# A linear-attention and feed-forward kernel: GpSimd's sums cut into parts, two casts on ScalarE, two sums and three stores moved

## The chip, the cores and the metric

One core of a Trainium2 chip runs the whole program. The metric is the time of one execution in microseconds on the device; three runs of the kernel before gave a median of 224.1 us (223.25 to 224.87). The profile is of one more execution, taken by the hardware profiler. The engines are named as the profile names them: PE is TensorE (matrix products; PEld is its weight loads), DVE is VectorE, ACT is ScalarE, POOL is GpSimd, and SP is SyncE, whose queue issues nearly all transfers.

## The reference, cut to what matters

```python
def _attn_ref(q, k, v, lam):                  # (4, 8, 768, 64) each, lam: one decay per head
    for b in range(nb):                       # blocks of 64 positions
        intra = einsum('bhic,bhjc->bhij', qb, kb) * Dmask      # decay lam**(i-j), causal
        intra = einsum('bhij,bhjd->bhid', intra, vb)
        inter = einsum('bhid,bhde->bhie', qb * lam_pow, kv_state)
        out[:, :, sl] = intra + inter
        kv_state = lam_block * kv_state + einsum('bhsd,bhse->bhde', kb_dec, vb)

def _moe_ref(x, w_a, w_b, w_out):             # x: 3072 tokens x 512, d_ff = 1536
    a = x @ w_a
    b = x @ w_b
    return a * b @ w_out
```

The attention's output, with its heads joined, is the x of the feed-forward part. Inputs and output are float32; the kernel multiplies in bfloat16.

## The kernel before, in words

The 3072 tokens are 24 units of 128 (four sequences of six blocks; the kernel takes blocks of 128). `GROUPS = (4, 1, 2, 4, 4, 4, 4, 1)` gathers them into eight groups, and the feed-forward part works on one group at a time. While it multiplies group g, the attention of later units is woven in, a piece at a time, at numbered slots. `PLAN[g]` lists by hand which piece goes at which slot of group g; `hook(slot)` emits them. What a piece's letters mean, as far as it matters here:

- `P`: prepare a unit. `prep_k` (L433) scales k and q by the decay on GpSimd (L411) and has SP issue the transpose by DMA (L439); `prep_v` (L444) casts v to bfloat16 on the engine that `VB_ENG` names (L428, L430) and then calls `pump` (L312), which lets SP issue the loads of a later unit. `PK` and `PV` are the two halves.
- `S`, `O2`, `V`: the scores of a unit with their masks (L467, L481, L482, L490), the outputs of two units (L507; L530 writes them to xT, the feed-forward part's input) and the update of the state.
- `W`: `store_kept` (L637) has SP store one of five early output rows that were kept in SBUF (L639). Rows 3 and 4 lie in one tile, rows 0, 1 and 2 in another, with the tag `zab`.
- `X`: `x_sums` (L730) forms for the next group the three sums z_sub, z_add and z_mix of quarters of xT.
- `SM`: `ab_sum` (L852), one of eight partial sums of a group's product tile `ab`. The sums go to a tile z with the tag `zab`, the same memory as the kept rows 0 to 2, or back into `ab`.
- `H`: `out_half` (L873), half of one product of the output.

Groups 3 to 6 use seven products in place of eight for each pair of blocks (`ffn_z`, L752): every product's operands are quarters of xT and of the weights, or their sums. A round n of six forms the seven products for one slice of columns of both a and b: product 1 goes to a PSUM bank U, 4 to a bank V, 5 and 2 or 3 add onto U, 6 onto V, and 0 goes to W. Product 4 reads z_sub, 5 reads z_mix, 6 and 0 read z_add, and product 2, the last, reads z_sub. ScalarE copies U and V to SBUF (L849), and DVE subtracts (L797, L805, L807, L809, L814). L807 must have read U before product 2 adds onto it (`last_product`, L772), which is done one round later; then ScalarE casts U (L774) and DVE multiplies a by b into rows n and n + 6 of `ab` (L776). A round has three slots, 3n to 3n + 2; at slot 3n + 1 of groups 3 and 4 the last product of round n - 1 has just been issued. In group 5 and 6 the outputs of the group before run at the same time (`joined`), and the last product of round n - 1 follows right after product 1.

`ab_sum(4, 0)` adds two column halves of rows 0 to 2 of `ab` (into z3), `ab_sum(4, 2)` subtracts in place in rows 0 to 2, reading rows 6 to 8 as well, and `ab_sum(4, 4)` goes on from it. `SUM_ENG` gives sum (4, 0) to DVE and (4, 2) to GpSimd; of the 24 sums of groups 4 to 6, GpSimd has 13, each of 3 x 256 elements a partition. `XS_ENG` gives z_add and z_mix of group 5 and all three sums of group 6 to GpSimd (1024, 1024 and 512 elements).

Every engine takes its instructions in the order in which they were issued, and so does SP's queue: a piece that waits holds all that stands behind it on its engine.

Of the kernel before, what the change touches and what calls it, by code (L numbers as in the profile page):

```python
# [22 lines left out]
def _bc(ap, dims):  # L23
# [73 lines left out]
VB_ENG = dict(enumerate(["pool"] * 7 +  # L97
                        ["dve"] * 3 +
                        ["pool"] * 5 +
                        ["dve"] * 2 +  # L100
                        ["act"] +
                        ["pool"] +
                        ["dve"] +
                        ["pool"] +
# [1 line left out]
SUM_ENG = {(3, 0): 'dve', (3, 1): 'dve', (3, 2): 'pool', (3, 3): 'dve', (3, 4): 'pool', (3, 5): 'pool', (3, 6): 'dve', (3, 7): 'dve', (4, 0): 'dve', (4, 1): 'pool', (4, 2): 'pool', (4, 3): 'pool', (4, 4): 'dve', (4, 5): 'pool', (4, 6): 'pool', (4, 7): 'pool', (5, 0): 'dve', (5, 1): 'dve', (5, 2): 'pool', (5, 3): 'pool', (5, 4): 'dve', (5, 5): 'pool', (5, 6): 'pool', (5, 7): 'dve', (6, 0): 'pool', (6, 1): 'dve', (6, 2): 'pool', (6, 3): 'dve', (6, 4): 'dve', (6, 5): 'pool', (6, 6): 'dve', (6, 7): 'dve'}  # L106
XS_ENG = {(3, 0): 'dve', (3, 1): 'dve', (3, 2): 'dve', (4, 0): 'dve', (4, 1): 'dve', (4, 2): 'dve', (5, 0): 'dve', (5, 1): 'pool', (5, 2): 'pool', (6, 0): 'pool', (6, 1): 'pool', (6, 2): 'pool'}
# [6 lines left out]
def kernel(  # L114
# [12 lines left out]
    B, H, S, D = q.shape  # L127
# [7 lines left out]
    KS = d_model // 128  # L135
# [61 lines left out]
    HN, NP = d_model // 2, FC // 2  # L197
# [209 lines left out]
    def eng_of(name):  # L407
        return nc.gpsimd if name == "pool" else nc.vector
# [314 lines left out]
    def x_tile():  # L723
        return xz_pool.tile([128, 2, 512], BF16, name="z_add", tag="xz")
# [5 lines left out]
    def x_sums(g):  # L730
        xT = gx[g]
        z_add = x_first.pop(g) if g in x_first else x_tile()
        add_half = lambda c: nc.vector.tensor_add(z_add[:, :, c], xT[:, 0:2, c], xT[:, 2:4, c])
        z_sub = xz_pool.tile([128, KS, 256], BF16, name="z_sub", tag="xz")
        z_mix = mix_pool.tile([128, 2, 256], BF16, name="z_mix", tag="z_mix")
        xz[g] = (z_add, z_sub, z_mix)
        if g == Z_GROUPS[0]:
            sub = lambda s: nc.vector.tensor_sub(z_sub[:, s], xT[:, s, 0:256], xT[:, s, 256:512])
            sub(slice(0, 2))
            nc.vector.tensor_add(z_mix, xT[:, 0:2, 0:256], xT[:, 2:4, 256:512])  # L740
            add_half(slice(256, 512))
            sub(slice(2, 4))
            return
        eng_of(XS_ENG[g, 0]).tensor_sub(z_sub, xT[:, :, 0:256], xT[:, :, 256:512])
        eng_of(XS_ENG[g, 1]).tensor_add(z_add, xT[:, 0:2, :], xT[:, 2:4, :])
        eng_of(XS_ENG[g, 2]).tensor_add(z_mix, xT[:, 0:2, 0:256], xT[:, 2:4, 256:512])

    fin = []
    pairs = [0]
    outs = {}  # L750
# [101 lines left out]
    def ab_sum(g, i):  # L852
        d = outs[g]
        if "z" not in d:
            d["z"] = sum_pool.tile([128, 2, NP, 256], BF16, name="zab", tag="zab")
        ab, z, j, h = d["ab"], d["z"], i // 2, i % 2
        lo, hi = h * NP // 2, (h + 1) * NP // 2
        a11, a12 = ab[:, lo:hi, :256], ab[:, NP + lo:NP + hi, :256]
        a21, a22 = ab[:, lo:hi, 256:], ab[:, NP + lo:NP + hi, 256:]
        z1, z3 = z[:, 0, lo:hi], z[:, 1, lo:hi]  # L860
        eng = eng_of(SUM_ENG[g, i])
        if j == 0:
            eng.tensor_add(z3, a11, a21)
        elif j == 1:
            eng.tensor_sub(a21, a22, a21)
        elif j == 2:
            eng.tensor_sub(z1, a11, a21)
        else:
            eng.tensor_sub(z1, a12, z1)
# [165 lines left out]
    for g, n in enumerate(GROUPS):  # L1035
# [6 lines left out]
        def hook(slot, plan=plan):  # L1042
            for name, us in plan.get(slot, ()):
# [9 lines left out]
                elif name == "W":  # L1053
                    store_kept()
                elif name == "WS":
                    weight_sum(us)
                elif name == "WO":
                    out_sum(us)
                elif name == "SM":
                    ab_sum(*us)  # L1060
                elif name == "H":
                    out_half(*us)
                elif name == "XA":
                    x_add_first(us)
                elif name == "X":
                    x_sums(us)
                elif name == "T":
                    piece_T(us)
                elif name == "S":
                    piece_S(us)  # L1070
                elif name == "VC":
                    kv_copy(us, kv["ps"], KV_ENG[us])
                elif name == "V":
                    piece_V(us)
                elif name == "O":
                    pieces_O((us,))
                elif name == "O2":
                    pieces_O(us)
                else:
                    pieces_O(us[:2], us[2:])  # L1080
# [41 lines left out]
```

## Time and profile before

| | us |
|---|---|
| median of three runs | 224.1 |
| the profiled execution | 223.99 |
| its span, first to last instruction | 222.3 |
| PE busy | 214.2 |
| DVE busy | 166.1 |
| ACT busy | 122.2 |
| POOL busy | 101.4 |
| PE waits on named engines from 82 us on (1.0, 0.3, 0.3, and some of 0.2) | about 2 |

Busy time is the union of an engine's instructions, and the granted clock of TensorE is 1.00 throughout. A line of a timeline reads: start, duration, engine, line of the code, operation, output and input, count; in brackets the idle time of that engine just before, and what ended it. Group 4's rounds run from about 117 to 141 us, group 5's to about 171, group 6's to about 202.

### The profile page before, as it was taken

Reading aid. Unit: us, or ns where it says so; the run is one execution under the profiler, and the core shown is the slowest. Engines: PE = TensorE matmul, PEld = TensorE weight load, DVE = VectorE, ACT = ScalarE, POOL = GpSimd, SP = SyncE. Lnnn points to the kernel's source line nnn. Section 1 sums busy time; section 2 is a strip of 40 time slices with the busy share of each in tenths; the row PEclk is TensorE's granted clock in tenths of the full one; section 3 lists DMA queues with packets and bytes.
Section 4 is the critical chain, followed back from the end, with each engine's and each line's share of the span. In section 5 each row is a group of like instructions: output and inputs, shape, how many; then the busy total and the mean of one; then the engine's idle time right before and its main releaser. Section 6 shows DMA issues by size and latency. Waiting matters only on the chain.

```text
span 222.3 us, 5600 instructions
## 1 busy us (share of the span) xinstructions
PE 214.2 (96%) x2225; PEld 158.8 (71%) x2235; DVE 166.1 (75%) x272; ACT 122.2 (55%) x249; POOL 101.4 (46%) x99
## 2 busy tenths in 40 slices
PE   7799999999999999999999999899999999999994
PEld 2376444448788658886547888688888888888994
DVE  0895673987868667989999879968688865777540
ACT  2586447028454267664356988676635566543322
POOL 6052003337795365533479519786417722051100
PEclk9999999999999999999999999999999999999999
DMA  3999999999999999999999999872021100112042
GB/s 107 332 245 354 354 386 355 272 222 208 223 196 190 217 188 232 192 288 186 193 254 195 266 230 254 140 131 49 1 86 59 52 0 3 49 47 97 0 145 94
DMA packets 99081, 39.42 MB, mean 177 GB/s; under 512 B 85488, under 2 KB 95088, under 8 KB 99056
## 3 DMA queue, kind: packets, MB, share of 16 engines
q1 hardware_dynamic: 98768, 39.00, 80.5%
q8 instruction: 17, 0.28, 0.6%
q10 hardware_dynamic: 288, 0.07, 0.1%
q14 instruction: 8, 0.07, 0.1%
HBM read 28.32 MB, written 6.29 MB: 156 GB/s over the span
## 4 chain that ended last, share of the span: by engine, by line
PE 68%; DMA 14%; DVE 8%; SPq 3%; issue 3%; ACT 2%; ACTq 0%; DVEq 0%
PE U L768 17%; PE op L890 12%; PE V L768 9%; DMA wst<-in_moe_w_b_dram 8%; PE op L655 5%; PE W L768 5%; PE a_ps L606 5%; PE b_ps L606 5%; PE o_ps L507 3%; DMA kf<-in_k_dram 3%; DMA k<-in_k_dram 3%; PE op L830 3%; PE kq L467 2%; DVE m L490 2%; SPq L360 1%
## 5 line engine op out<-in xcount | busy, mean ns | idle before, releaser
L849 ACT COPY u<-U 128x512 f32<-128x512 f32 x48 | 28.4, 591 | 17.3 <-PE U L768 17.3
L411 POOL TENSOR_TENSOR qk<-kf,lp_k 128x512 bf16<-128x512 f32 x18 | 20.2, 1124 | 26.3 <-DMA kf<-in_k_dram 19.9
L633 DVE TENSOR_TENSOR ab<-a_sb,b_ps 128x128 bf16<-128x128 bf16 (+2 forms) x48 | 19.5, 418 | 15.4 <-ACT a_sb L615 11.0
L776 DVE TENSOR_TENSOR ab<-oab 128x1024 bf16<-128x1024 bf16 x24 | 20.4, 848 | 10.7 <-ACT oab L774 10.5
L606 PE MATMUL b_ps<-xT,wb_sb 128*128 128x128 bf16 (+2 forms) x192 | 27.5, 272 | 0.2 <-DVE wb_sb L251 0.2
L606 PE MATMUL a_ps<-xT,wa_sb 128*128 128x128 bf16 (+2 forms) x198 | 27.4, 267 | 0.1
L490 DVE TENSOR_TENSOR m<-kq,lotri 128x512 bf16<-128x512 f32 x40 | 25.6, 680 | 0.9 <-PE kq L467 0.8
L615 ACT CAST a_sb<-a_ps 128x128 bf16<-128x128 f32 (+2 forms) x48 | 17.1, 375 | 13.8 <-PE a_ps L606 13.1
L411 POOL TENSOR_TENSOR qk<-qf,lp_q 128x512 bf16<-128x512 f32 x20 | 23.0, 1149 | 2.6 <-DMA qf<-in_q_dram 2.1
L655 PE MATMUL op<-wo_sb,ab 128*128 128x512 bf16 (+2 forms) x114 | 22.0, 335 | 0.5 <-issue 0.3
L606 PEld LDWEIGHTS <-wa_sb 128*128 128x128 bf16 x200 | 16.7, 98 | 6.0 <-POOL wa_sb L246 0.2
L768 PEld LDWEIGHTS <-wz_a 128*128 128x128 bf16 x192 | 18.1, 98 | 3.6 <-issue 0.3
L768 PEld LDWEIGHTS <-wz_b 128*128 128x128 bf16 x192 | 18.7, 98 | 2.2
L606 PEld LDWEIGHTS <-wb_sb 128*128 128x128 bf16 x192 | 15.7, 98 | 6.3 <-DVE wb_sb L251 0.3
L530 ACT CAST xT<-o_ps 128x512 bf16<-128x512 f32 (+1 forms) x24 | 12.2, 554 | 12.8 <-PE o_ps L507 12.7
L768 PE MATMUL U<-xT,wz_a 128*128 128x256 bf16 x96 | 18.3, 272 | 0.0
L768 PE MATMUL U<-xT,wz_b 128*128 128x256 bf16 x96 | 18.3, 272 | 0.0
L430 POOL CAST vb<-vf 128x512 bf16<-128x512 f32 x14 | 10.1, 724 | 17.0 <-DMA vf<-in_v_dram 14.6
L768 PEld LDWEIGHTS <-wa_sb 128*128 128x128 bf16 x144 | 13.4, 98 | 4.6 <-issue 1.8
L807 DVE TENSOR_TENSOR oab<-U,u 128x512 bf16<-128x512 f32 x24 | 16.3, 680 | 0.6 <-PE U L768 0.6
L774 ACT CAST oab<-U 128x512 bf16<-128x512 f32 x24 | 14.2, 591 | 3.9 <-PE U L768 3.9
L655 PEld LDWEIGHTS <-ab 128*128 128x128 bf16 x120 | 10.1, 98 | 8.3
(130 smaller groups left out, 454.4 us busy)
## 6 DMA issues: line engine op xcount, KB each, us to landing
vf<-in_v_dram SPq DMA_DIRECT2D x24, 256.0 KB, 5.4
qf<-in_q_dram SPq DMA_DIRECT2D x20, 256.0 KB, 4.8
kf<-in_k_dram SPq DMA_DIRECT2D x20, 256.0 KB, 4.6
out_dram<-o_sb SPq DMA_DIRECT2D x18, 256.0 KB, 2.7
wst<-in_moe_w_a_dram SPq DMA_DIRECT2D x6, 512.0 KB, 8.5
wst<-in_moe_w_b_dram SPq DMA_DIRECT2D x6, 512.0 KB, 8.9
wst<-in_moe_w_out_dram SPq DMA_DIRECT2D x6, 512.0 KB, 10.6
out_dram<-o_kept SPq DMA_DIRECT2D x5, 256.0 KB, 4.5
```

What stands on the lines that cost most here:

```text
L411: eng_of(eng).tensor_mul(dst.rearrange("p (c b) d -> p b c d", b=2), x[:].rearrange("p (b c) d -> p b c d", b=2), lp.rearrange("p (b c) o ...
L490: nc.vector.tensor_mul(m, kq[i], lotri_bc)
L606: nc.tensor.matmul(ps[:, lo:hi], lhsT=w_sb[:, s, f * 128:(f + 1) * 128], rhs=xT[:, s, lo:hi], start=(s == 0), stop=(s == KS - 1), skip_gro ...
L615: nc.scalar.copy(a_sb[:, :gt], ps[:, :gt])
L633: nc.vector.tensor_mul(ab[:, f, :gt], a_sb[:, :gt], ps[:, :gt])
L655: nc.tensor.matmul(op[:, lo:hi], lhsT=ab[:, f, t * 128:(t + 1) * 128], rhs=wo_sb[:, f, lo:hi], start=(f == 0), stop=(f == FC - 1))
L768: nc.tensor.matmul(ps[:, k, :], lhsT=wt[:, s, n * 128:(n + 1) * 128], rhs=rhs[i][:, s, :], start=(fresh and k == 0 and s == 0), stop=True, ...
L774: nc.scalar.copy(oab[:, 0], U)
L776: nc.vector.tensor_mul(ab[:].rearrange("p (h i) (t c) -> p h i t c", h=2, t=2)[:, :, n], o5[:, :, :, 0, :], o5[:, :, :, 1, :])
L807: nc.vector.tensor_sub(oab[:, 1], U, v1)
L849: nc.scalar.copy(t, ps)
L890: nc.tensor.matmul(ps[:, t, :], lhsT=lhs[p][:, n, t * 128:(t + 1) * 128], rhs=rhs[:, n, :], start=fresh, stop=True, skip_group_check=True)
```

## The change

Four things change. `x_sums` and `ab_sum` cut what GpSimd does into instructions of 256 elements (z_sub and z_mix by rows, z_add by 128 columns of two rows, the sums of `ab` by rows); sums on DVE stay whole. The casts of v of units 15 and 16 go from DVE to ScalarE. In `PLAN`, sums (4, 0) and (4, 2) go from slots 16 and 17 of group 4 to slots 10 and 12. The stores of kept rows 0, 1 and 2 go from slot 23 of group 3 and slots 2 and 5 of group 4 to slot 18 of group 3, ahead of the update of unit 13, and to slot 4 of group 4, between the two halves of unit 19's preparation; and the halves `PV` of units 15 and 21 come one and three slots after their `PK`.

```diff
     3: [...
-        (15, 'P', 15), (17, 'WO', 0), (17, 'S', 14), (18, 'V', 13), (18, 'WO', 1),
+        (15, 'PK', 15), (16, 'PV', 15), (17, 'WO', 0), (17, 'S', 14), (18, 'W', None), (18, 'V', 13), (18, 'WO', 1),
...
-        (23, 'W', None), (24, 'WO', 2), (25, 'WO', 4), (25, 'X', 4)],
-    4: [(0, 'S', 16), (1, 'V', 15), (2, 'W', None), (3, 'S', 17), (4, 'O2', (15, 16)), (4, 'P', 19), (5, 'W', None),
-        (6, 'P', 20), (6, 'S', 18), (10, 'O2', (17, 18)), (10, 'X', 5), (11, 'S', 19),
-        (13, 'P', 21), (16, 'SM', (4, 0)), (17, 'SM', (4, 2)), (17, 'PK', 22), (17, 'S', 20),
+        (24, 'WO', 2), (25, 'WO', 4), (25, 'X', 4)],
+    4: [(0, 'S', 16), (1, 'V', 15), (3, 'S', 17), (4, 'O2', (15, 16)), (4, 'PK', 19), (4, 'W', None), (4, 'W', None), (4, 'PV', 19),
+        (6, 'P', 20), (6, 'S', 18), (10, 'SM', (4, 0)), (10, 'O2', (17, 18)), (10, 'X', 5), (11, 'S', 19),
+        (12, 'SM', (4, 2)), (13, 'PK', 21), (16, 'PV', 21), (17, 'PK', 22), (17, 'S', 20),
         (17, 'SM', (4, 4))],
...
 VB_ENG = ...
-                        ["dve"] * 2 +
-                        ["act"] +
+                        ["act"] * 3 +
...
 def x_sums(g):
...
+        def parts(i, n, step, one):
+            w = step if XS_ENG[g, i] == "pool" else n
+            for lo in range(0, n, w):
+                one(eng_of(XS_ENG[g, i]), lo, lo + w)
+
+        parts(0, KS, 1, lambda eng, lo, hi: eng.tensor_sub(
+            z_sub[:, lo:hi], xT[:, lo:hi, 0:256], xT[:, lo:hi, 256:512]))
+        parts(1, 512, 128, lambda eng, lo, hi: eng.tensor_add(
+            z_add[:, :, lo:hi], xT[:, 0:2, lo:hi], xT[:, 2:4, lo:hi]))
+        parts(2, 2, 1, lambda eng, lo, hi: eng.tensor_add(
+            z_mix[:, lo:hi], xT[:, lo:hi, 0:256], xT[:, 2 + lo:2 + hi, 256:512]))
...
 def ab_sum(g, i):
...
+        lo, hi = i % 2 * NP // 2, (i % 2 + 1) * NP // 2
+        step = 1 if SUM_ENG[g, i] == "pool" else hi - lo
+        for at in range(lo, hi, step):
+            ab_sum_part(g, i, at, at + step)
```

`ab_sum_part(g, i, lo, hi)` is the old body of `ab_sum` for rows lo to hi.

More of the change, by code (lines that the diff above doesn't have):

```diff
@@ L743, in x_sums @@
             return
-        eng_of(XS_ENG[g, 0]).tensor_sub(z_sub, xT[:, :, 0:256], xT[:, :, 256:512])
-        eng_of(XS_ENG[g, 1]).tensor_add(z_add, xT[:, 0:2, :], xT[:, 2:4, :])
-        eng_of(XS_ENG[g, 2]).tensor_add(z_mix, xT[:, 0:2, 0:256], xT[:, 2:4, 256:512])
+        def parts(i, n, step, one):
[8 more added lines that the diff above has]
+            z_mix[:, lo:hi], xT[:, lo:hi, 0:256], xT[:, 2 + lo:2 + hi, 256:512]))
     fin = []
@@ L855, in ab_sum, with ab_sum_part @@
             d["z"] = sum_pool.tile([128, 2, NP, 256], BF16, name="zab", tag="zab")
-        ab, z, j, h = d["ab"], d["z"], i // 2, i % 2
-        lo, hi = h * NP // 2, (h + 1) * NP // 2
+        lo, hi = i % 2 * NP // 2, (i % 2 + 1) * NP // 2
+        step = 1 if SUM_ENG[g, i] == "pool" else hi - lo
+        for at in range(lo, hi, step):
+            ab_sum_part(g, i, at, at + step)
+    def ab_sum_part(g, i, lo, hi):
+        d = outs[g]
+        ab, z, j = d["ab"], d["z"], i // 2
         a11, a12 = ab[:, lo:hi, :256], ab[:, NP + lo:NP + hi, :256]
```

## The prediction

> **What bounds the kernel now.** I read the page's first lines for the bound, then TensorE's waits from 82 us on, where the change acts, and then the timeline of each engine around the few places where TensorE stands.
>
> ```profile
> span 222.3 us, 5600 instructions
> PE 214.2 (96%) x2225; PEld 158.8 (71%) x2235; DVE 166.1 (75%) x272; ACT 122.2 (55%) x249; POOL 101.4 (46%) x99
> ```
> ```profile
> PE U L768 <- DVE oab L807: 1.0, 2, 0.8
> ```
> ```profile
> PEld L768 <- DVE z_mix L746: 0.3, 1, 0.3
> PEld L768 <- DVE oab L814: 0.3, 1, 0.3
> ```
>
> TensorE is busy for 96% of the span, and from 82 us on all that it waits for by name is 1.0 + 0.3 + 0.3 us (the other rows are "issue" and 0.2 us ones). So no rearrangement of helpers can win more than about 1.6 us, 0.7%. What they can lose has no such cap. The change moves work among the helpers, so the question is where a helper is just in time for TensorE. There are two tight places, both where one group of tokens hands over to the next.
>
> The first hand-over, from group 4 to group 5, in the timelines of DVE, POOL and PE:
>
> ```profile
> 131.80 0.69 DVE L776 TENSOR_TENSOR ab<-oab 128x1024 bf16<-128x1024 bf16 x1 [0.58 <-ACT oab L774]
> 132.82 0.69 DVE L744 TENSOR_TENSOR z_sub<-xT 128x1024 bf16<-128x1024 bf16 x1 [0.33 <-ACT xT L530]
> 136.43 0.93 DVE L776 TENSOR_TENSOR ab<-oab 128x1024 bf16<-128x1024 bf16 x1
> 137.28 0.68 DVE L807 TENSOR_TENSOR oab<-U,u 128x512 bf16<-128x512 f32 x1
> 139.55 0.69 DVE L776 TENSOR_TENSOR ab<-oab 128x1024 bf16<-128x1024 bf16 x1 [0.40 <-ACT oab L774]
> 140.16 0.55 DVE L863 TENSOR_TENSOR zab<-ab 128x768 bf16<-128x768 bf16 x1
> 140.62 0.69 DVE L807 TENSOR_TENSOR oab<-U,u 128x512 bf16<-128x512 f32 x1
> ```
> ```profile
> 132.87 2.63 POOL L745 TENSOR_TENSOR z_add<-xT 128x1024 bf16<-128x1024 bf16 x1 [4.50 <-ACT xT L530]
> 138.22 1.04 POOL L411 TENSOR_TENSOR qk<-qf,lp_q 128x512 bf16<-128x512 f32 x1
> 140.79 1.64 POOL L865 TENSOR_TENSOR ab<-ab 128x768 bf16<-128x768 bf16 x1 [1.53 <-DVE zab L863]
> ```
> ```profile
> 138.19 0.38 PE L768 MATMUL U<-z_sub,wa_sb 128*128 128x256 bf16 x2
> 141.36 0.38 PE L768 MATMUL U<-z_sub,wa_sb 128*128 128x256 bf16 x2 [0.81 <-DVE oab L807]
> ```
>
> The 0.81 us wait at 141.36 is the largest. DVE does its first sum (L863, 140.16) ahead of the subtraction L807 that frees U. But one step earlier DVE is hardly better off: its L807 of 137.28 ends at 137.96, and TensorE needs it at 138.19, 0.23 us later.
>
> The second hand-over, from group 5 to group 6:
>
> ```profile
> 168.78 2.13 POOL L744 TENSOR_TENSOR z_sub<-xT 128x1024 bf16<-128x1024 bf16 x1 [1.41 <-ACT xT L530]
> 170.87 2.58 POOL L745 TENSOR_TENSOR z_add<-xT 128x1024 bf16<-128x1024 bf16 x1
> 173.40 1.47 POOL L746 TENSOR_TENSOR z_mix<-xT 128x512 bf16<-128x512 bf16 x1
> ```
> ```profile
> 170.06 1.40 DVE L776 TENSOR_TENSOR ab<-oab 128x1024 bf16<-128x1024 bf16 x1 [0.79 <-ACT oab L774]
> 172.76 1.10 DVE L867 TENSOR_TENSOR zab<-ab 128x768 bf16<-128x768 bf16 x1
> 174.57 0.85 DVE L776 TENSOR_TENSOR ab<-oab 128x1024 bf16<-128x1024 bf16 x1
> ```
> ```profile
> 174.97 0.38 PE L768 MATMUL U<-z_mix,wz_a 128*128 128x256 bf16 x2
> ```
>
> GpSimd's third sum, z_mix, ends at 173.40 + 1.47 = 174.87, and TensorE reads it at 174.97. The rows also show how the two engines exclude each other: L776 asked at 170.06, took 1.40 us instead of 0.69, and ended 0.55 us after GpSimd's sum ended (170.91). GpSimd's next sum then took 2.58 us instead of 2.13. L867 did the same at the next boundary (asked 172.76, GpSimd ended 173.45, DVE ended 173.86). A waiting DVE sum slips in between two GpSimd instructions and costs GpSimd about 0.45 us.
>
> **The change part by part.** *GpSimd's sums in parts.* What does a sum of 256 elements cost? No row has one. Two sizes stand undisturbed: 768 elements 1.64 us (140.79), 1024 elements 2.13 us (168.78). The line through them gives 0.49 us per 256 elements and 0.17 us fixed, so 0.66 us a part. In a pair of sums the second starts 0.05 us before the first's recorded end:
>
> ```profile
> 154.97 3.23 POOL L869 TENSOR_TENSOR zab<-ab,zab 128x768 bf16<-128x768 bf16 x2 [1.88 <-PE op L890]
> ```
>
> That is 3.23 - 1.64 = 1.59 us of spacing for 1.64 us. So a part occupies about 0.61 us. The other end is strict proportion, 2.13 / 4 = 0.53 us. I take 0.61, because both rows are of this operation and type and only the length is extrapolated. In sentences that the rest can do without: the Trainium skill, GPSIMD Engine Reference, section 3.1, gives about 2.6 cycles an element for a two-input sum and 4497 ns for 2048 elements, from which I estimate 0.06 us fixed for an instruction. By it the seven extra instructions below would cost 0.4 us rather than 0.9, and the term of 1.2 us would be 0.7. Its rate is off, though (2.28 us for 1024 elements where the row has 2.13), so the rows' line decides.
>
> For group 6's three sums that is ten parts, 9 x 0.61 + 0.66 = 6.2 us, against 2.13 + 2.13 + 1.15 (512 elements by the same line) - 0.1 = 5.3 us: 0.9 us more on GpSimd. Then DVE's L776 of 174.57, which now waits for the end of z_mix, comes before its last part and takes its 0.45 us. So z_mix is ready near 174.87 + 0.9 + 0.45 = 176.2, and TensorE, in order, waits for it: 1.2 us later than 174.97. Bounds: 0.0 us (proportional parts, L776 behind the last part) and 1.8 us (one more DVE sum in between). I take **+1.2**. The gain on the other side, L776 and L867 waiting for one part, lets product 4 start up to 0.3 us earlier (the L814 row above), but the very next product needs z_mix, so it is worth nothing.
>
> The thirteen partial sums of a and b in three parts each cost 3 x 0.66 - 0.1 - 1.64 = 0.24 us more. The tightest reader:
>
> ```profile
> 204.80 1.64 POOL L867 TENSOR_TENSOR zab<-ab 128x768 bf16<-128x768 bf16 x1 [6.75 <-DVE ab L865]
> ```
> ```profile
> 207.50 0.82 PE L890 MATMUL op<-wy,zab 128*128 128x256 bf16 x6
> ```
>
> Slack 1.06 us, so **0** there; without it, 0.24 us.
>
> *First two sums of group 4 at slots 10 and 12.* Slot 10 comes right after the product L776 of 131.80, the earliest place, since that writes the last row summed. DVE then has 0.33 us free (the wait at 132.82), and the sum takes 0.55 us, so z_sub asks some 0.15 us later. Now GpSimd's first part of z_add, from 132.87, may be ahead of it: up to 0.6 us. L482 and L776 of 136.43 meet parts as well. DVE's L807 of 137.28 then comes 0.2 to 0.9 us later against 0.23 us of slack: TensorE loses 0 to 0.7 us at 138.19, I take 0.4. At 141.36 the sum is gone from before L807: 0.46 us back (140.16 to 140.62). But GpSimd has the second sum (1.9 us in parts) ahead of unit 21's two scalings, which in the run before ended at 139.26; they now run until about 141.4, so L776 of 139.55, which met an idle GpSimd, waits for part of 1.04 us. I take 0.3 of it, which makes 0.4 - 0.46 + 0.3, about **+0.25**, between -0.5 (all cover holds) and +1.3. The transposes and scores behind unit 21 have room: its scores run at
>
> ```profile
> 152.21 0.40 PE L467 MATMUL kq<-qkT 64*128 64x128 bf16 x8
> ```
> ```profile
> 139.28 2.28 SPq L439 DMA_TRANSPOSE qkT<-qk  x1
> ```
>
> and a transpose 2 us later still lands some 6 us ahead. Unit 21's cast and the loads of unit 23, three slots later, have the same room.
>
> *Late stores ahead.* The first sum overwrites the tile that keeps rows 0 to 2, so it needs their stores landed:
>
> ```profile
> 124.36 0.43 SPq L639 DMA_DIRECT2D out_dram<-o_kept  x1
> 125.33 0.66 SPq L639 DMA_DIRECT2D out_dram<-o_kept  x1
> 126.09 1.50 SPq L439 DMA_TRANSPOSE qkT<-qk  x1
> 128.64 2.08 SPq L187 DMA_DIRECT2D qf<-in_q_dram  x1
> 131.60 1.03 SPq L639 DMA_DIRECT2D out_dram<-o_kept  x1
> ```
> ```profile
> DMA to landing us min/median/max: 4.1/4.5/5.6
> ```
>
> The last store, issued at 131.60, would land at 136.1, far too late, hence the move. SP's queue runs back to back here, so the order decides. Row 0 now goes ahead of unit 16's transpose and delays what follows by 0.4 to 1.3 us (SP stands about 1 us for a store near 112, which takes it up). The two others follow unit 19's transpose, which itself moves up to about 125.0: stores at 126.5 and 127.2 to 128, the last landed between 131.3 and 133.6. The sum wants it at 132.4. I take **0**, the middle being just in time; up to 1.2 us of DVE's queue otherwise, of which most reaches L807. The loads of unit 21 go out about 1 us later; GpSimd reads them only after the moved sum, so 0.
>
> *Two casts on ScalarE.* DVE loses 0.41 and 1.26 us of casts around 103 and 109.5; ScalarE has room in both:
>
> ```profile
> 106.15 0.59 ACT L774 CAST oab<-U 128x512 bf16<-128x512 f32 x1 [2.41 <-PE U L768]
> 110.26 1.07 ACT L530 CAST xT<-o_ps 128x512 bf16<-128x512 f32 x2 [2.10 <-PE o_ps L507]
> ```
>
> against about 0.6 us a cast; without that room, 0.6 us on the snapshots. What it wins is the 0.3 us for z_mix L746 at the start of group 4: **-0.15**, between 0 and -0.3.
>
> Sum: 1.2 + 0.25 + 0 - 0.15 = +1.3 us. The profiled execution took 223.99 us (span 222.3), 0.1 us under the median of the three runs, 224.1; so **225.3**.
>
> **The rivals.**
> 1. *The parts free DVE.* DVE's two-input sums wait for a quarter of a sum instead of a whole one; L776 and L867 lost 0.7 and 0.55 us. If z_mix is not late (proportional parts), what is left are the gains: 223.99 - 0.46 - 0.3 - 0.3 = 222.9, the three places where TensorE waits in the rows above. For it: the 1.40 and 1.10 rows. Against it: the 0.1 us of slack of z_mix. The Trainium skill, SBUF — State Buffer, section "Who interferes with whom", has it as a rule that the one that starts first holds the shared port for the whole instruction, which is what parts shorten; the trace agrees (1.40 against 0.69 us), and the rule speaks for this rival.
> 2. *The stores hold DVE*, slower. If SP gains nothing (transpose still at 126.1) and the last store follows at 128.7 and takes 5.6 us, it lands at 134.3, 1.9 us after the sum is due. DVE's queue stands, L807 with it, and beyond the 0.23 us of slack TensorE loses about 1.6 us on top of the sum: 226.9. It decides from a landing after 132.6 on.
> 3. *The move does nothing*: what L807 gains is lost to GpSimd's later scalings, and z_mix is late by half: 224.5.
>
> **How the numbers follow.** The forecast (z_mix late) 0.52, rival 1 0.22, rival 2 0.16, rival 3 0.10. The likeliest gives 225.3. The range goes from rival 1, 222.9, to rival 2 and the forecast's own upper bounds, 227.2. A change of 1% (2.2 us) is about what a measurement of this kernel can tell from none: faster than 221.9 needs more than TensorE's waits hold, 0.03; slower than 226.3 is rival 2 and the upper part of the forecast, 0.19; the rest, 0.78, within.
>
> **What would show it.** A part on GpSimd: 0.61 us of spacing if right, 0.53 if rival 1. z_mix of group 6 ending about 176 and TensorE waiting about 1 us for it between the V and the U products: the forecast. DVE's first sum waiting on a DMA to out_dram: rival 2. No L807 wait at the hand-over 4 to 5, and none new before it: the move works. What would make me wrong is a GpSimd part much costlier than the line says, or GpSimd winning the boundary over a waiting DVE.

## The result and the profile after

The changed kernel takes 226.3 us where the prediction had 225.3 (222.9 to 227.2): against the kernel before the ratio is 1.0109 [1.0062, 1.0156], so about 2.4 us are lost and none won. Four executions gave 226.25, 226.34, 229.95 and 230.69; the last two were disturbed, and such executions (the profiled one of e6 is another) are left out of every ratio here. Six more of the same kernel on another chip gave 1.0127 [1.0083, 1.0171] (e9 below). So it is slower, by an amount that lies on the 1% bound: the prediction had the direction, and about half of the size.

The profiled execution took 226.34 us. The page's first lines, and TensorE's waits from 82 us on. The lines of the code have moved: the helper lines L768, L776, L807 and L849 of before are L775, L783, L814 and L856 here, and the sums L744 to L746, L863 to L867 are L748 to L752, L876 to L880.

```profile
span 224.3 us, 5652 instructions
PE 214.1 (95%) x2235; PEld 158.6 (71%) x2235; DVE 163.1 (73%) x270; ACT 123.5 (55%) x251; POOL 106.7 (48%) x136
```
```profile
PE U L775 <- ACT u L856: 1.5, 1, 1.5
PE U L775 <- DVE oab L814: 1.3, 2, 0.7
PE U L775 <- POOL z_mix L752: 0.8, 1, 0.8
```

TensorE does the same work (214.1 us against 214.2). GpSimd has 37 instructions and 5.3 us more, DVE 3.0 us less, of which the two moved casts are 1.7: DVE is freer, and it doesn't help. Where one wait of 0.8 us stood there are now four, in three places: a new one on ScalarE, two at the hand-over from group 4 to group 5, and one for z_mix at the hand-over from group 5 to group 6.

The first hand-over in the timelines of DVE and POOL:

```profile
131.92 0.69 DVE L783 TENSOR_TENSOR ab<-oab 128x1024 bf16<-128x1024 bf16 x1 [0.31 <-ACT oab L781]
132.95 0.56 DVE L876 TENSOR_TENSOR zab<-ab 128x768 bf16<-128x768 bf16 x1 [0.34 <-DMA out_dram<-o_kept]
133.42 1.16 DVE L748 TENSOR_TENSOR z_sub<-xT 128x1024 bf16<-128x1024 bf16 x1
...
137.23 1.18 DVE L783 TENSOR_TENSOR ab<-oab 128x1024 bf16<-128x1024 bf16 x1
138.34 0.68 DVE L814 TENSOR_TENSOR oab<-U,u 128x512 bf16<-128x512 f32 x1
...
140.36 1.13 DVE L783 TENSOR_TENSOR ab<-oab 128x1024 bf16<-128x1024 bf16 x1 [0.15 <-ACT oab L781]
141.41 0.68 DVE L814 TENSOR_TENSOR oab<-U,u 128x512 bf16<-128x512 f32 x1
```
```profile
128.60 1.73 POOL L750 TENSOR_TENSOR z_add<-xT 128x256 bf16<-128x256 bf16 x2
132.98 2.13 POOL L750 TENSOR_TENSOR z_add<-xT 128x256 bf16<-128x256 bf16 x2 [2.65 <-ACT xT L529]
135.07 1.29 POOL L752 TENSOR_TENSOR z_mix<-xT 128x256 bf16<-128x256 bf16 x2
136.33 2.61 POOL L878 TENSOR_TENSOR ab<-ab 128x256 bf16<-128x256 bf16 x3
```

The moved sum (L876) stands for 0.34 us until a kept row's store has landed. The subtraction z_sub behind it starts 0.60 us later than before and meets GpSimd, which has z_add at 132.98: 1.16 us instead of 0.69. L783 of 137.23 and of 140.36 meet the moved second sum and GpSimd's scalings. So L814 ends at 139.02 and 142.09, and TensorE, which waits for both, stands twice where it stood once:

```profile
139.06 0.38 PE L775 MATMUL U<-z_sub,wa_sb 128*128 128x256 bf16 x2 [0.60 <-DVE oab L814]
```

Counted from the end of the last product's issue to the start of the next, the two gaps in TensorE's stream are 0.75 and 0.90 us, where the one of before was 0.97: 0.68 us more. (Each is some 0.16 us longer than the wait that is named, and all gaps below are counted in this way.) The two parts of z_add at 128.60 are new: in parts, z_add needs only those columns of xT that are there already.

The second hand-over, in the timelines of POOL, DVE and PE:

```profile
166.51 1.93 POOL L878 TENSOR_TENSOR ab<-ab 128x256 bf16<-128x256 bf16 x3 [7.39 <-DVE zab L876]
169.08 3.00 POOL L748 TENSOR_TENSOR z_sub<-xT 128x256 bf16<-128x256 bf16 x4 [0.64 <-ACT xT L529]
172.04 2.87 POOL L750 TENSOR_TENSOR z_add<-xT 128x256 bf16<-128x256 bf16 x4
174.87 1.74 POOL L752 TENSOR_TENSOR z_mix<-xT 128x256 bf16<-128x256 bf16 x2
```
```profile
170.84 0.71 DVE L783 TENSOR_TENSOR ab<-oab 128x1024 bf16<-128x1024 bf16 x1 [0.79 <-ACT oab L781]
...
173.54 0.83 DVE L880 TENSOR_TENSOR zab<-ab 128x768 bf16<-128x768 bf16 x1
...
175.34 0.75 DVE L783 TENSOR_TENSOR ab<-oab 128x1024 bf16<-128x1024 bf16 x1 [0.36 <-ACT oab L781]
```
```profile
176.66 0.27 PE L775 MATMUL U<-z_mix,wz_a 128*128 128x256 bf16 x1 [0.80 <-POOL z_mix L752]
```

DVE's sums meet short parts now: L783 took 0.71 us where it took 1.40. But z_mix ends at 174.87 + 1.74 = 176.61, and TensorE's stream has a gap of 0.96 us for it.

The third place lies at the start of group 4, in the timelines of ACT and SP:

```profile
110.61 0.59 ACT L649 COPY o_sb<-op 128x512 f32<-128x512 f32 x1
117.89 0.58 ACT L649 COPY o_sb<-op 128x512 f32<-128x512 f32 x1 [4.09 <-DMA out_dram<-o_sb]
```
```profile
107.21 0.91 SPq L638 DMA_DIRECT2D out_dram<-o_kept  x1
112.29 0.87 SPq L650 DMA_DIRECT2D out_dram<-o_sb  x1
```

The same rows in the kernel before:

```profile
112.00 0.59 ACT L650 COPY o_sb<-op 128x512 f32<-128x512 f32 x1
117.23 0.59 ACT L650 COPY o_sb<-op 128x512 f32<-128x512 f32 x1 [2.05 <-PE op L830]
```
```profile
112.61 0.36 SPq L651 DMA_DIRECT2D out_dram<-o_sb  x1
```

ScalarE copies the last output row of group 3 (L649) into one of three buffers, and the one it needs still holds the row that it copied at 110.61. That copy ended at 111.20, but SP issued its store only at 112.29, 1.09 us later; before, 0.03 us lay between the two. The store of kept row 0 (L638, at 107.21) now stands ahead in SP's queue, and ScalarE's copy comes 1.39 us earlier than before. ScalarE goes on at 117.89, 5.6 us after the store's issue; the copies of U behind it (L856) are late, and TensorE has a gap of 1.67 us.

These gaps and the ones of before account for the span. Lost: 1.67 (ScalarE), 0.68 (first hand-over), 0.96 less a gap of 0.26 that stood there before, and a new one of 0.28 at 179.18. Won: about 0.65 in small gaps between 101 and 106 us (0.33 of it at 102.14), and 0.76 at group 3's first product (82.06 against 82.82), before anything that the change touches: by chance, then. That makes +1.9 of the +2.0 us of span. (The profile before also shows TensorE idle for 0.32 us at 110.41, but one record of a product is missing there: TensorE's lead over the kernel before is 1.39 us ahead of that place and behind it.) A further 0.35 us lies outside the span: 226.34 - 224.3 against 223.99 - 222.3.

### The profile page after: what moved, and what is told of

Same layout as the page of the kernel before. It is cut to its first block, busy times and chain, and to the rows that moved or that the text cites. A ratio compares the mean times of both kernels' runs of the same rounds, so it can differ in the third digit from the quotient of the medians.

```text
span 224.3 us, 5652 instructions
## 1 busy us (share of the span) xinstructions
PE 214.1 (95%) x2235; PEld 158.6 (71%) x2235; DVE 163.1 (73%) x270; ACT 123.5 (55%) x251; POOL 106.7 (48%) x136
## 4 chain that ended last, share of the span: by engine, by line
PE 68%; DMA 11%; SPq 7%; POOL 5%; DVE 4%; issue 3%; ACT 1%; POOLq 0%; DVEq 0%; ACTq 0%
PE U L775 13%; PE op L903 12%; PE op L654 10%; PE a_ps L605 10%; PE b_ps L605 9%; PE V L775 6%; DMA kf<-in_k_dram 4%; SPq L186 4%; PE W L775 3%; PE o_ps L506 3%; DMA wst<-in_moe_w_a_dram 3%; SPq L438 2%; DMA out_dram<-o_kept 2%; DMA q<-in_q_dram 2%; PE kq L466 2%
## 5 line engine op out<-in xcount | busy, mean ns | idle before, releaser
L856 ACT COPY u<-U 128x512 f32<-128x512 f32 x48 | 28.4, 591 | 17.6 <-PE U L775 17.5
L410 POOL TENSOR_TENSOR qk<-kf,lp_k 128x512 bf16<-128x512 f32 x18 | 20.9, 1161 | 29.9 <-DMA kf<-in_k_dram 12.7
L783 DVE TENSOR_TENSOR ab<-oab 128x1024 bf16<-128x1024 bf16 x24 | 19.3, 802 | 11.1 <-ACT oab L781 11.0
L410 POOL TENSOR_TENSOR qk<-qf,lp_q 128x512 bf16<-128x512 f32 x20 | 22.1, 1107 | 3.7 <-DMA qf<-in_q_dram 3.3
L654 PE MATMUL op<-wo_sb,ab 128*128 128x512 bf16 (+2 forms) x120 | 22.8, 337 | 0.0
L775 PEld LDWEIGHTS <-wz_a 128*128 128x128 bf16 x192 | 18.2, 98 | 5.2 <-issue 2.0
L775 PEld LDWEIGHTS <-wz_b 128*128 128x128 bf16 x192 | 18.7, 98 | 3.2 <-issue 1.0
L775 PE MATMUL U<-xT,wz_a 128*128 128x256 bf16 x96 | 18.3, 272 | 0.0
L775 PE MATMUL U<-xT,wz_b 128*128 128x256 bf16 x96 | 18.3, 272 | 0.0
L814 DVE TENSOR_TENSOR oab<-U,u 128x512 bf16<-128x512 f32 x24 | 16.3, 680 | 1.6 <-PE U L775 1.6
L775 PEld LDWEIGHTS <-wa_sb 128*128 128x128 bf16 x144 | 13.4, 98 | 4.8 <-issue 2.0
L429 POOL CAST vb<-vf 128x512 bf16<-128x512 f32 x14 | 9.5, 682 | 14.4 <-DMA vf<-in_v_dram 13.8
```

The source lines that it names most:

```text
L410: eng_of(eng).tensor_mul(dst.rearrange("p (c b) d -> p b c d", b=2), x[:].rearrange("p (b c) d -> p b c d", b=2), lp.rearrange("p (b c) o ...
L654: nc.tensor.matmul(op[:, lo:hi], lhsT=ab[:, f, t * 128:(t + 1) * 128], rhs=wo_sb[:, f, lo:hi], start=(f == 0), stop=(f == FC - 1))
L775: nc.tensor.matmul(ps[:, k, :], lhsT=wt[:, s, n * 128:(n + 1) * 128], rhs=rhs[i][:, s, :], start=(fresh and k == 0 and s == 0), stop=True, ...
L783: nc.vector.tensor_mul(ab[:].rearrange("p (h i) (t c) -> p h i t c", h=2, t=2)[:, :, n], o5[:, :, :, 0, :], o5[:, :, :, 1, :])
L814: nc.vector.tensor_sub(oab[:, 1], U, v1)
L856: nc.scalar.copy(t, ps)
```

## The experiments

Theory A: the loss is what the prediction added up, z_mix late and the hand-over from 4 to 5 a little worse. Theory B: it is the store of row 0, moved ahead, that makes ScalarE stand at group 4's start. Theory C: the two moved sums cost much more than the 0.25 us given to them. (The recorded expectations letter their theories anew in each run; the text between them means these three, unless it says otherwise.) Each kernel is compared with the kernel before on the same chip. The last two columns split the difference of the means into what lies between first and last instruction, and what lies outside.

| | what it is | ratio [95%] | in the span, us | outside, us |
|---|---|---|---|---|
| e1 | the change, row 0's store late | 1.0090 [1.0059, 1.0122] | +1.88 | +0.23 |
| e2 | parts alone | 1.0054 [1.0035, 1.0074] | +1.15 | +0.16 |
| e3 | casts alone | 0.9984 [0.9963, 1.0004] | -0.34 | 0.00 |
| e4 | all moves alone | 1.0135 [1.0096, 1.0174] | +3.16 | +0.02 |
| e5 | moved stores and halves alone | 0.9998 [0.9953, 1.0044] | +0.10 | -0.01 |
| e6 | parts, z_mix first in group 6 | 1.0010 [0.9976, 1.0045] | -0.10 | +0.13 |
| e7 | all moves, z_mix first in group 5 | 1.0133 [1.0079, 1.0188] | +2.74 | -0.01 |
| e8 | casts, and sum (4, 0) one slot later | 1.0055 [1.0018, 1.0092] | +1.05 | 0.00 |
| e9 | the change again | 1.0127 [1.0083, 1.0171] | +2.46 | +0.33 |
| e10 | the change, z_mix first in group 6 | 1.0079 [1.0039, 1.0120] | +1.58 | +0.36 |
| e11 | the change, sums back at 16 and 17 | 1.0086 [1.0058, 1.0114] | +1.54 | +0.33 |
| e12 | casts and parts, z_mix first | 1.0042 [1.0020, 1.0065] | +0.58 | +0.33 |

**e1: row 0's store back at its old place**, the rest of the change kept.

```diff
-        (15, 'PK', 15), (16, 'PV', 15), (17, 'WO', 0), (17, 'S', 14), (18, 'W', None), (18, 'V', 13), (18, 'WO', 1),
+        (15, 'PK', 15), (16, 'PV', 15), (17, 'WO', 0), (17, 'S', 14), (18, 'V', 13), (18, 'WO', 1),
...
-        (24, 'WO', 2), (25, 'WO', 4), (25, 'X', 4)],
+        (23, 'W', None), (24, 'WO', 2), (25, 'WO', 4), (25, 'X', 4)],
```

> The changed kernel with one store put back: kept row 0 at slot 23 of group 3 instead of slot 18. Theory A (the 1.5 us that TensorE waits for ScalarE at the start of group 4 comes from the moved store: it delays the store of group 3's first output row, whose buffer ScalarE's copy of the fourth row needs): ScalarE's wait of 4.1 us on a DMA to out_dram shrinks under 1 us, TensorE's wait goes, about 224.9 us. Theory B (the two casts hold ScalarE): the wait stays, 226.3 us.

ScalarE's wait is gone, as B of this section has it. The pair is a clean one, as ScalarE's first copy comes at 110.62 here and at 110.61 there; SP issues its store 0.03 us after the copy's end:

```profile
111.23 0.73 SPq L650 DMA_DIRECT2D out_dram<-o_sb  x1
```

But the time, 225.7 us where 224.9 was expected, is no different from the change's within the intervals. The moved sum is due 1.7 us earlier than in the change, the other kept rows' stores go out only 0.9 us earlier, and the sum waits longer for them:

```profile
131.66 0.74 DVE L876 TENSOR_TENSOR zab<-ab 128x768 bf16<-128x768 bf16 x1 [0.71 <-DMA out_dram<-o_kept]
```
```profile
PE U L775 <- DVE oab L814: 2.1, 3, 1.1
PE U L775 <- POOL z_mix L752: 0.8, 1, 0.8
```

The waits for L814 grew from 1.3 to 2.1 us. Of the 1.67 us won at 117 us, 0.95 were given back at 134 to 142 (gaps of 0.56, 0.78 and 1.27 for 0.75 and 0.90).

**e2: the parts alone** (the new `x_sums` and `ab_sum`, `PLAN` and `VB_ENG` as before).

> The kernel before, with GpSimd's sums in parts and nothing else. Theory A (each wait has its own cause; the parts make z_mix of group 6 late): TensorE waits 0.5 to 1.2 us for z_mix at the step from group 5 to 6 and nowhere else anew, 224.3 to 224.8 us. Theory C (GpSimd's longer stream of instructions is what costs, all over): 225.5 us or more, new waits in other places too. Rival 1 of the prediction (the parts free DVE): under 223.5 us.

```profile
174.84 1.74 POOL L753 TENSOR_TENSOR z_mix<-xT 128x256 bf16<-128x256 bf16 x2
```
```profile
PE U L776 <- DVE oab L815: 1.0, 2, 0.8
PE U L776 <- POOL z_mix L753: 0.8, 1, 0.8
```

The wait for z_mix is there and that of the first hand-over is as it was before. The mean is 1.3 us up, of which 1.15 in the span, near the predicted term of 1.2. Not all of it is z_mix: the gap for it is 0.95 us, and one of 0.26 that stood there before is gone, which leaves 0.7. A gap of 0.30 us is new at 153.96, just behind DVE's mask L482, which took 1.07 us in place of 0.41; so the sums of `ab` in parts, which the prediction put at 0, probably cost this.

**e3: the casts alone.**

```diff
-                        ["dve"] * 2 +
-                        ["act"] +
+                        ["act"] * 3 +
```

> The kernel before, with the casts of v of units 15 and 16 on ScalarE and nothing else. Theory A: TensorE's small gaps between 101 and 111 us go (0.3 + 0.2 + 0.3 us), about 223.2 us, no new wait for ScalarE. Theory B: TensorE waits 1 us or more for ScalarE at the start of group 4, 225 us.

0.35 us faster, with an interval that takes in no difference, and no new wait for ScalarE. The predicted -0.15 is neither shown nor refuted. The small gaps that were expected to go did not go in its profile: TensorE still waits 0.2 us twice at 104.6 and 105.2, where DVE's product L775 took 1.56 us.

**e4: the moves alone** (the new `PLAN`; sums whole, casts on DVE).

> The kernel before, with the moves in the plan alone (stores, two sums, halves of preparations); sums whole, casts on DVE. Theory A: the wait for ScalarE at the start of group 4 is there but smaller, 0.5 to 1.2 us, as TensorE comes there later; at the step from group 4 to 5 the wait changes by less than 0.5 us; none for z_mix of group 6; 224.3 to 225 us. Theory C: 223.5 to 224 us, as the parts are not in it.

This is the largest loss of any single part, about 3 us, and both expectations missed it. DVE and POOL:

```profile
131.68 0.56 DVE L863 TENSOR_TENSOR zab<-ab 128x768 bf16<-128x768 bf16 x1
132.15 2.61 DVE L744 TENSOR_TENSOR z_sub<-xT 128x1024 bf16<-128x1024 bf16 x1
```
```profile
132.00 2.21 POOL L745 TENSOR_TENSOR z_add<-xT 128x1024 bf16<-128x1024 bf16 x1 [4.49 <-ACT xT L530]
```
```profile
PE U L768 <- DVE oab L807: 3.0, 5, 1.1
```

In the kernel before, z_sub asked at 132.82, 0.05 us ahead of z_add, and took 0.69 us. In e4 the moved sum keeps DVE until 132.24, z_add has been running since 132.00, and z_sub is done only at 134.76, half a microsecond after z_add's end at 134.21. No store held the moved sum in this execution. TensorE then has four gaps between 135 and 143 us (1.17, 0.70, 0.58 and 1.27, the second for L797), 3.7 us where 1.0 stood; two of the five waits for L807 come before 105 us.

**e5: the moved stores and halves alone**, the sums left at slots 16 and 17.

> The kernel with the moves alone, but the two sums back at slots 16 and 17: only the stores and the halves of the preparations of units 15, 19 and 21 are moved. Theory A (the moved sum, which pushes DVE's z_sub behind GpSimd's z_add, costs nearly all of what the moves cost): 223.3 to 224.2 us, z_sub of group 5 takes 0.7 us again, no waits of TensorE for L807 between 130 and 138 us. Theory B (the moved stores cost it, by delays in SP's queue and in the transfers): 225.5 us or more.

No difference, and z_sub is as short as before:

```profile
134.07 0.69 DVE L744 TENSOR_TENSOR z_sub<-xT 128x1024 bf16<-128x1024 bf16 x1 [0.33 <-ACT xT L530]
```

So what e4 loses comes with the two sums, not with the stores alone. What the stores do to a sum that needs them landed can't show here, as the sums are back.

**e6: parts, with z_mix ahead of z_add for group 6.** If the late z_mix is the loss of e2, this takes it away at no cost, since product 5 reads z_mix ahead of products 6 and 0, which read z_add.

```diff
-        parts(1, 512, 128, lambda eng, lo, hi: eng.tensor_add(
+        add = lambda: parts(1, 512, 128, lambda eng, lo, hi: eng.tensor_add(
             z_add[:, :, lo:hi], xT[:, 0:2, lo:hi], xT[:, 2:4, lo:hi]))
+        if g != 6:
+            add()
         parts(2, 2, 1, lambda eng, lo, hi: eng.tensor_add(
             z_mix[:, lo:hi], xT[:, lo:hi, 0:256], xT[:, 2 + lo:2 + hi, 256:512]))
+        if g == 6:
+            add()
```

> The kernel with the parts alone, with z_mix ahead of z_add among GpSimd's sums for group 6. Theory A (what the parts cost is z_mix of group 6 being late): TensorE's wait of about 1 us for z_mix goes, z_add takes no place as the last one, 223.6 to 224.0 us against 224.8. Theory C (the parts cost by their number, in many small waits): 224.5 us or more.

The wait for z_mix is gone, and most likely the loss of the parts with it: 1.0010 against 1.0054 for e2 (on different chips; the intervals overlap from 1.0035 to 1.0045). Its profile, of an execution of 226.91 us where the ten in the ratio have a mean of 224.2, shows something else:

```profile
PE U L780 <- ACT u L861: 2.4, 1, 2.4
```

This is the wait at group 4's start, in a kernel whose stores are all at their old places. SP's queue is late here too: it issues the row's store 2.01 us after ScalarE's copy. So B's cause, the moved store, isn't the only way to it.

**e7: the moves, with z_mix ahead of z_add in group 5**, so that DVE might meet a shorter sum.

```diff
-        eng_of(XS_ENG[g, 1]).tensor_add(z_add, xT[:, 0:2, :], xT[:, 2:4, :])
+        add = lambda: eng_of(XS_ENG[g, 1]).tensor_add(z_add, xT[:, 0:2, :], xT[:, 2:4, :])
+        if g != 5:
+            add()
         eng_of(XS_ENG[g, 2]).tensor_add(z_mix, xT[:, 0:2, 0:256], xT[:, 2:4, 256:512])
+        if g == 5:
+            add()
```

> The kernel with the moves alone, with GpSimd's z_mix (512 elements) ahead of its z_add (1024) for group 5. Theory A (DVE's z_sub, pushed back by the moved sum, waits for the whole GpSimd sum that started 0.15 us ahead of it): z_sub takes 1.6 us in place of 2.6, TensorE's waits for L807 between 130 and 140 us fall by about 1 us together, 225.3 to 225.8 us against 226.5. Theory B (the stores): 226.5 us, unchanged.

A miss: as slow as e4. The moved sum (4, 0), L867 here, waited for a store, then met z_mix, and z_sub met z_add:

```profile
132.84 1.55 DVE L867 TENSOR_TENSOR zab<-ab 128x768 bf16<-128x768 bf16 x1 [0.40 <-DMA out_dram<-o_kept]
134.31 2.60 DVE L744 TENSOR_TENSOR z_sub<-xT 128x1024 bf16<-128x1024 bf16 x1
```

Here another order of GpSimd's whole sums only changed which of DVE's instructions meet them. It supports C's mechanism, but it found no cure.

**e8: the casts, and sum (4, 0) one slot later** (an idea from the 0.81 us wait of before: let L807 go ahead of the sum).

```diff
-        (13, 'P', 21), (16, 'SM', (4, 0)), (17, 'SM', (4, 2)), (17, 'PK', 22), (17, 'S', 20),
+        (13, 'P', 21), (17, 'SM', (4, 0)), (17, 'SM', (4, 2)), (17, 'PK', 22), (17, 'S', 20),
```

> The kernel with the two casts on ScalarE, and sum (4, 0) one slot later than before (17 in place of 16), behind the subtraction L807 instead of ahead of it; nothing else is changed. Theory A (the 0.81 us that TensorE waits at the step from group 4 to 5 is the sum's 0.46 us and what is left of L807): the wait falls to 0.2 to 0.4 us, 222.6 to 222.9 us against 223.2 with the casts alone. Rival: GpSimd's second sum, now later, runs into DVE's next product and gives it back, 223.2 us.

The wait fell, as expected, and a new one took its place behind it:

```profile
PE op L889 <- DVE ab L775: 0.8, 1, 0.8
PE U L767 <- DVE oab L806: 0.6, 2, 0.3
```

Slower by 0.55%, worse than both expectations. The recorded rival's mechanism is what the rows show, at a higher price: against e3, DVE's first sum starts 1.4 us later (141.10), so does GpSimd's second, which needs it (141.73), DVE's next sum L866 stands 0.56 us for that one and meets GpSimd (1.38 us for 0.82), and the product L775 behind it ends 1.4 us later (0.2 of each 1.4 is only that this execution runs later by then). This hand-over has no room for a sum that is put off.

**e9: the change again**, for its own spread.

> The changed kernel unchanged, to stand beside the three others on one chip. Theory A (two terms: the moved sum at the step from group 4 to 5, and z_mix of group 6): ratio 1.009 to 1.012. If TensorE's wait for ScalarE at the start of group 4 belongs to the change (Theory S, the store of row 0), it is in this profile again, 1 to 2 us; if it is a chance of the transfers, it may be missing.

```profile
PE U L775 <- DVE oab L814: 1.5, 3, 0.7
PE U L775 <- POOL z_mix L752: 0.8, 1, 0.8
```
```profile
117.78 0.59 ACT L649 COPY o_sb<-op 128x512 f32<-128x512 f32 x1 [2.05 <-PE op L837]
```
```profile
113.16 0.53 SPq L650 DMA_DIRECT2D out_dram<-o_sb  x1
```

Here the wait on ScalarE is missing, though the row's store was issued 0.9 us later than in the first profile: it went out 0.03 us after ScalarE's copy, which came later too, and landed within the 4.6 us to 117.78. The other two places are as they were (gaps of 0.70, 0.90 and 0.96 us), and this execution, 226.5 us, is no faster. That is chance: its group 3 began at 83.31, 1.25 us later than in the first, and from there on it is 1.05 us shorter. (In the profiles of all the kernels here that point lies between 81.9 and 83.8 us, though no edit touches what comes before it.) The ratio, 1.0127, lies just above the 1.009 to 1.012 expected.

**e10: the change with z_mix ahead of z_add for group 6** (e6's edit), **e11: the change with the two sums back**, each to take one term out.

```diff
-        (6, 'P', 20), (6, 'S', 18), (10, 'SM', (4, 0)), (10, 'O2', (17, 18)), (10, 'X', 5), (11, 'S', 19),
-        (12, 'SM', (4, 2)), (13, 'PK', 21), (16, 'PV', 21), (17, 'PK', 22), (17, 'S', 20),
+        (6, 'P', 20), (6, 'S', 18), (10, 'O2', (17, 18)), (10, 'X', 5), (11, 'S', 19),
+        (13, 'PK', 21), (16, 'PV', 21), (16, 'SM', (4, 0)), (17, 'SM', (4, 2)), (17, 'PK', 22), (17, 'S', 20),
```

> The changed kernel with z_mix ahead of z_add among GpSimd's sums for group 6. Theory A: TensorE's 0.96 us for z_mix goes, about 1 us less than the changed kernel on this chip, ratio 1.005 to 1.008. Rival (the time is given back later): no difference.

> The changed kernel with the two sums of group 4 back at slots 16 and 17; parts, casts and moved stores stay. Theory A: the waits for L814 at 138 and 141 us (0.75 and 0.90) become one of 0.8 to 1.0, about 0.7 us less, ratio 1.004 to 1.007. Theory S: the wait for ScalarE at the start of group 4 is still there and the ratio stays above 1.008.

The waits of e10, then of e11:

```profile
PE U L779 <- DVE oab L818: 2.1, 3, 1.1
PE U L779 <- ACT u L860: 0.9, 1, 0.9
```
```profile
PE U L775 <- POOL z_mix L752: 0.8, 1, 0.8
PE U L775 <- DVE oab L814: 0.8, 1, 0.8
```

In each, the wait that the edit aims at is gone or single again, and the mean span is 0.9 us below e9's. The intervals overlap with e9's, so the 0.9 us are likely, not shown. e10's ratio is as expected, e11's 1.0086 lies above the 1.004 to 1.007 of its Theory A. In e11 ScalarE stands 0.33 us for the store at group 4's start, which TensorE doesn't feel.

**e12: casts and parts with z_mix first, nothing moved**: the version that the experiments pointed to.

> The kernel before with the two casts on ScalarE and the sums in parts, z_mix of group 6 ahead of z_add; stores and sums where they were. Theory A: both costly terms are out and the casts' gain is in, ratio 0.996 to 0.999, TensorE waits only at the step from group 4 to 5 (0.8 us). Theory C (many parts cost in themselves): 1.002 or more.

A miss. The profiled execution, 223.91 us, has only the wait of the kernel before:

```profile
PE U L779 <- DVE oab L818: 0.8, 1, 0.8
```

Yet the twelve runs are 0.4% slower than before. 0.33 us of it lies outside the span; the 0.58 us inside have no place in the one profile, whose span of 221.9 us is 0.4 under the mean of the twelve. No version is shown to beat the kernel before; the casts alone (0.9984) and the stores alone (0.9998) can't be told from it.

## Why the prediction was right, and where its sizes were off

**GpSimd's parts: right.** A part alone takes 0.67 us and the spacing is (1.93 - 0.67) / 2 = 0.63 us, for 0.66 and 0.61 in the prediction. The single part, from e2:

```profile
167.75 0.67 POOL L879 TENSOR_TENSOR ab<-ab 128x256 bf16<-128x256 bf16 x1
```

Strict proportion (0.53), the premise of rival 1, is refuted. The 0.06 us fixed that the prediction estimated from the Trainium skill, GPSIMD Engine Reference, section 3.1, is too low for these short sums: the rows give 0.67 - 0.49 = 0.18 us for a single one. z_mix of group 6 ended at 176.61 for a predicted 176.2, and its two parts took 1.74 us where 0.63 + 0.67 = 1.30 would be undisturbed: DVE's product came in between, as forecast. The gap in TensorE's stream is 0.96 us, or 0.7 net of the 0.26 that stood there before, for a term of 1.2, since TensorE came to the hand-over later too. So the 1.15 us of e2 agrees better than the mechanism does, and part of that is luck. With z_mix first the named wait goes in three profiles (e6, e10, e12); the time went with it in e6, and not wholly in e12. DVE's faster sums bought nothing, as argued.

**The moved sums: the step that was too small.** The prediction took 0.4 us for the first place, 138.19, and -0.46 + 0.3 for the second, 141.36: +0.25. In the profile after, the first place costs 0.75, and the second is 0.90 against 0.97, so -0.07 for -0.16: +0.68; e11 against e9 says 0.9. Most of what is missing is at the first place. L807 was to come "0.2 to 0.9 us later" and came 1.06 later (it ends at 139.02 instead of 137.96): z_sub starts 0.60 us later and not 0.15, 0.34 of that because the moved sum stood for a store, and it takes 0.47 us longer behind a part, within the "up to 0.6 us". (0.12 us is only that the whole kernel runs so much later by then.) At the second place L783 met GpSimd (1.13 us against 0.69), which ate nearly all of the 0.46. The prediction also didn't see how near the move is to something worse: with whole sums it costs 3 us (e4), because z_sub had won its turn by 0.05 us. The Trainium skill, SBUF — State Buffer, "Who interferes with whom", says that issue order decides which of the two blocks; the trace agrees (2.61 against 0.69 us). The prediction named that rule for rival 1 alone, at the second hand-over; at the first it is the price of the move.

**The stores: not 0, in two ways.** Moved without the sums they cost nothing (e5). But rival 2's sign is there: the moved sum stood for the last store until 132.95, past the 132.6 from which that rival was to decide. It stood 0.34 us, inside the bounds but not the 0 that was taken, and not the 1.9 us that rival 2's price rests on; it is 0.28 in e9, 0.40 in e7, 0.71 in e1 and nothing in e4. Second, the prediction let the 1 us for which SP stands near 112 take up the delay from row 0's store. In the profile after SP is 0.6 us later there and ScalarE's copy 1.39 us earlier, so nothing is left of that 1 us, and the output row's store goes out 1.09 us late.

**The casts: not decided.** -0.35 us, with an interval from -0.8 to +0.1, for -0.15. The gap at 102.14 is gone in the profile after, but it wasn't the cast's: it waits for L807 of 101.74, which DVE ran ahead of its cast at 102.94.

**Not in the sum at all:** first, 0.33 us outside the span (2.05 us around it instead of 1.72, in every run of the change). It comes with the parts (0.16 in e2) and is larger with the casts beside them (e12), though the casts alone have none; what it is, no profile here shows. Second, ScalarE's wait for a store at group 4's start. ScalarE stands there in four of the fourteen profiles, the four in which SP issued that store late: 1.09 us after the copy's end in the first profile, 2.01 in e6, 0.25 in e10 and 0.59 in e11. TensorE lost 1.5, 2.4, 0.9 and 0 us by it. In the ten others the store went out within 0.03 us, and there is no such wait. The moved store can bring it, as e1 against the change shows, but it is not the only way (e6), and with it there is often none (e4, e5, e7, e9). In three of the four the store also took longer to land than the 4.6 us that bound it elsewhere (5.6 to 5.9), which no run here explains. How often the wait comes in the timed runs stays open.

Together: 1.15 (e2, in the span) + 0.68 (first hand-over) - 0.34 (e3) + 0.33 (outside) = 1.8 us, for a measured 2.4 to 2.8. That is more than the predicted 1.3, but the rest isn't assigned; the wait on ScalarE in some executions is a candidate and no more. So the direction and both hand-overs were foreseen, but that the time lies inside the stated range owes something to the range's width. The parts don't add up by themselves either: 1.15 + 3.16 - 0.34 = 4.0 us in the span if done singly, 2.5 together (e9). The change's own parts seem to repair half of what its moves break: z_sub meets a part (1.16 us) and not a whole sum (2.61).

## What to carry to other kernels

Before cutting an engine's work into parts, look for the reader with the least slack behind the last part: the extra fixed time adds up there, and the producers are best put in the order in which they are read (e6, e10). Before moving an instruction by half a microsecond on an engine that shares a port, look at which neighbour it passes: who asks first decides, and here a lead of 0.05 us carried 2 us of waiting. The 0.8 us at the end of a chain without slack were not won by putting one link later (e8), because the next link was as tight. And idle time of a queue that issues transfers is no reserve by itself: it must lie ahead of the transfer that can't be late.

## What the runs showed of the hardware

- GpSimd's sums and scalings and DVE's sums and products of bfloat16 tiles exclude each other by whole instructions, and what counts is the order of asking: z_sub took 0.69 us when it came 0.05 us ahead of GpSimd's sum, 2.61 behind a whole one, 1.16 behind a quarter. DVE's subtractions that read a PSUM bank are not held: L814 of 138.34 took 0.68 us in the middle of GpSimd's work (136.33 to 140.95), and all 72 of them in that profile took 0.67 to 0.69.
- A waiting DVE sum takes the boundary between two parts: four parts take 3.00 us with one such visit, where 0.67 + 3 x 0.63 = 2.56 would be undisturbed, so about 0.44 us a visit, as for whole sums (0.31 in the next four, of 2.87 us).
- The landing of one and the same kind of store, a row of the output, differed by a microsecond between executions (5.6 us from issue in one profile, under 4.6 in the next), which together with a store issued 1.09 us late made a wait of 1.5 us on TensorE.
- The time around the span isn't constant between kernels: 1.72 us before, 2.05 after, steady to within 0.15 in a kernel.
